# Moving value casts, a carry and a residual add in the issue order of a fused linear-attention and highway kernel

## The chip, the cores and the metric

The kernel runs on one core of a Trainium2 chip. The metric is the device time of one execution in microseconds (us); where several runs exist, their median.

## The reference

Eight batches of eight heads, 576 rows and 64 columns go through an attention without a score matrix, and the result through a highway layer of width 512:

```
q_s = exp(q) / sum over columns          (the maximum cancels)
k_s = exp(k) / sum over rows
kv  = k_s^T v                            (64 x 64 for each head)
x   = q_s kv                             (4608 x 512, heads side by side)
H   = max(x w_h, 0);  T = sigmoid(x w_t + b_t)
out = T*H + (1-T)*x
```

Inputs and output are float32; inside, the kernel works in float16 with float32 sums in PSUM.

## The kernel before, in words

**Tiles.** A batch lies in SBUF as 128 partitions by 4 head groups by 9 row blocks by 64 columns. Eight of the nine row blocks go through the highway layer batch by batch (column c = 0 to 7); the ninth blocks of all batches are collected and make two last columns of their own, c = 8 and 9. The layer works on transposed x, so each column has four output blocks ob = 0 to 3 of 128 features. Two batches form a pair g, whose rows leave the chip together.

**Steps of a batch b.** `exp_half` (L179, ScalarE) takes the exponential of half of q or k. `cast_v` (L189, GpSimd) converts half of the values to float16; batches 1 and 2 use `cast_v_head` (L197), a quarter at a time, on GpSimd and ScalarE. `q_sums` (L230, VectorE) sums exp(q) over the columns, half a batch at a time; `q_sums_tree` (L240) does the same by two adds and a shorter sum. `q_recip` (L251, VectorE) inverts the sums, and `q_scale_p` (L262, GpSimd) multiplies exp(q) by them, in two pieces (row blocks 0 to 3 and 4 to 8; batches 1 and 2 in three). The scaled q is turned by TensorE and copied back by VectorE (`q_trans`, L266, three pieces), for batches 6 and 7 by transposing DMAs on SP's queue (`q_turn`, L287). `kv_half` (L206, TensorE) forms k^T v, which needs the cast values and exp(k) but not the scaled q; `kv_norm` (L219, VectorE) normalizes it. `x_pair` (L331, TensorE, then a copy by ScalarE) needs both kv and the turned q.

**Steps of a block (c, ob).** `gate` (L375): four matmuls (`pt`), then tanh on ScalarE. `carry` (L386): four matmuls (`ph`), then one VectorE operation (`dd`, L401) that merges relu and x. `blend` (L406, VectorE, L409) multiplies the two. `pt` and `ph` share four PSUM banks, so a later gate or carry waits until an earlier `dd` or blend has read its bank. `add_x` (L417, at L421) adds x to the blended block on GpSimd; the blocks that `late` (L419) names are added on VectorE. `out_tile` (L436, eight per pair) turns the result back by one TensorE matmul for each block and, for blocks not in `added(g)` (L414), adds x by a second matmul.

**Order of the work.** No planner is at work: each engine executes in the order in which the program emits its instructions. The emission order is a list of start-up steps (L585), followed by `events` (L500), a table sorted by a hand-given position: block (c, ob) has its gate at 8c + 2ob, its carry at one more, its blend at two more. A batch b's steps stand around p = 8(b - 1), with offsets by batch (L543 to L579): `s0`, `s1` for the sums, `sc` for the scaling, `tr` for the turns, `kv`, and `x`. Steps of equal position keep the order of the source.

```
            s = p + {3: 0, 4: 0}.get(b, -0.5)
            at(s, E(exp_half, b, "k", 0), E(cast_v, b, 0))
            at(s + 0.9, E(cast_v, b, 1))
            at(s + 1, E(exp_half, b, "k", 1))
...
            4: ((3, 4, 4.9), (4.5, 4.5), (5.9, 6.9)),
...
        E(exp_half, 2, "q", 0), E(q_sums_tree, 2, 0), E(exp_half, 2, "q", 1),
        E(q_sums_tree, 2, 1), E(q_recip, 2),
```

Of the kernel before, what the change touches and what calls it, by code (L numbers as in the profile page):

```python
# [18 lines left out]
def kernel(  # L19
# [10 lines left out]
    nc = tc.nc  # L30
    B, H, S, D = q.shape
# [128 lines left out]
    def two_banks(name, dt=FP32):  # L160
        return ps_2.tile([P, 2, 2048 // (4 if dt is FP32 else 2)], dt, tag="q2", name=name)
# [202 lines left out]
    def views(c):  # L364
        if c >= B:
            h = slice(4 * (c - B), 4 * (c - B) + 4)
            return lambda k_: x9[:, k_, h], lambda k_: g9[:, k_, h]
        g, b2 = c // 2, c % 2
        if g not in gT:
            gT[g] = gp.tile([P, 4, NM, 2, 64], FP16, tag="g", name=f"g_{g}")  # L370
        return lambda k_: xT[g][:, k_, :, b2, :], lambda k_: gT[g][:, k_, :, b2, :]
# [39 lines left out]
        )  # L411


    added = lambda g: ((0, 1), (0, 1, 2), (0, 1, 2), (0, 1, 2, 3))[g]  # L414
    added9 = lambda g: (0, 1, 2, 3) if g < 2 else (0, 1)

    def add_x(c, ob):  # L417
        xv, gv = views(c)
        late = ob == (3 if c == B - 1 else 2) and c % 2 and c < B  # L419
        eng = nc.vector if late else nc.gpsimd  # L420
        eng.tensor_add(gv(ob), gv(ob), xv(ob))  # L421

# [79 lines left out]
    def at(p, *fs):  # L502
        events.setdefault(p, []).extend(fs)

    E = lambda f, *a: (lambda: f(*a))

    for c in range(1, B + 2):
        for ob in range(4):
            p = 8 * c + 2 * ob
# [6 lines left out]
    for g in range(B // 2):  # L516
        p = 16 * (g + 1)
# [6 lines left out]
    p = 8 * B + 8  # L524
# [1 line left out]
    at(p + 4, E(tile9, 1, 4))  # L526
    at(p + 8, E(tile9, 2, 3), E(tile9, 3, 3), E(last9))

    at(8, E(cast_v_head, 2, 0, nc.gpsimd), E(q_scale_p, 2, 0, 4), E(q_scale_p, 2, 4, 8))
    at(8.2, E(x_left, 1))  # L530
    at(16.2, E(x_left, 2))
    at(9, E(exp_half, 2, "k", 0))
    at(10, E(cast_v_head, 2, 1, nc.scalar), E(exp_half, 2, "k", 1))
    at(10.5, E(blend, 0, 3))
    at(12.5, E(add_x, 0, 0), E(add_x, 0, 1), E(add_x, 1, 0))
    at(14.5, E(add_x, 1, 1))
    for c in range(2, B + 2):
        for ob in added(c // 2) if c < B else added9(2 * (c - B)):
            at(8 * c + 2 * ob + (2.5 if c < B - 1 else 2.02), E(add_x, c, ob))
    at(11, E(cast_v_head, 2, 2, nc.gpsimd), E(cast_v_head, 2, 3, nc.scalar))  # L540
    at(11, E(q_scale_p, 2, 8, N9))
    for b in range(2, B):
        p = 8 * (b - 1)  # L543
        if b > 2:
            e0, e1, s0, s1, sc = {
                3: (-2.6, -1.6, -1.1, -0.1, 1),
                4: (-5.5, -4.5, -2.8, -1.5, -1.4),
                5: (-5, -4, -3.4, -2.7, -2.6),
                6: (-6, -5, -3.95, -3.1, -3),
                7: (-6, -5, -3.95, -3.1, -3),  # L550
            }.get(b, (-5, -4, -3.9, -2.9, -2.8))
            at(p + e0, E(exp_half, b, "q", 0))
            at(p + e1, E(exp_half, b, "q", 1))
            at(p + s0, E(q_sums, b, 0))
            at(p + s1, E(q_sums, b, 1), E(q_recip, b))
            at(p + sc, E(q_scale_p, b, 0, 4))
            at(p + sc + (0.6 if b > 5 else 0), E(q_scale_p, b, 4, N9))
            s = p + {3: 0, 4: 0}.get(b, -0.5)
            at(s, E(exp_half, b, "k", 0), E(cast_v, b, 0))
            at(s + 0.9, E(cast_v, b, 1))  # L560
            at(s + 1, E(exp_half, b, "k", 1))
        tr, kv, x = {
            2: ((5, 6, 7.1), (4, 6.2), (6.5, 7.2)),
            3: ((4, 4.9, 4.95), (4, 4), (5.9, 6.9)),
            4: ((3, 4, 4.9), (4.5, 4.5), (5.9, 6.9)),
        }.get(b, ((2, 3, 4), (4, 4), (5, 6)))
        if b in turned:
            at(p - 1.05, E(q_turn, b, 0, 4), E(q_turn, b, 4, N9))
        else:
            for i in range(3):  # L570
                home = (lambda: two_banks("pq_t", FP16)[:, 0]) if b < 4 and i == 2 else None
                at(p + tr[i], E(q_trans, b, i, home))
        at(p + kv[0], E(kv_half, b, 0))
        if b == 2:
            at(p + kv[0], E(kv_norm, b, 0, 1))
            at(p + kv[1], E(kv_half, b, 1), E(kv_norm, b, 1, 2))
        else:
            at(p + kv[1], E(kv_half, b, 1), E(kv_norm, b))
        homes = (nat_bank, single) if b == 2 else None  # L579
        at(p + x[0], E(x_pair, b, 0, "AA" if b == 2 else "A", b > 2, homes))  # L580
        at(p + x[1], E(x_pair, b, 1, "AV" if b == 2 else "A", b > 2, homes))
# [3 lines left out]
    for f in [  # L585
        E(warm_up, 24),
        E(exp_half, 0, "q", 0), E(q_sums, 0, 0),
        E(exp_half, 0, "q", 1), E(q_sums, 0, 1),
        E(q_recip, 0), E(q_scale_v, 0, 0, 4), E(q_scale_v, 0, 4, N9),
        E(exp_half, 0, "k", 0), E(cast_v, 0, 0),  # L590
        E(exp_half, 0, "k", 1), E(cast_v, 0, 1),
        E(q_trans, 0, 0), E(q_trans, 0, 1, lambda: two_banks("pq_0_1", FP16)[:, 0]), E(warm_up, 2), E(q_trans, 0, 2, lambda: nat_bank("pq_0_2", FP16)),
        E(warm_up, 6),
        E(kv_half, 0, 0), E(gate_bias), E(warm_up, 2), E(kv_half, 0, 1), E(kv_norm, 0),
        *[E(cast_weight, "t", k_, (nc.vector, nc.gpsimd)[k_ % 2]) for k_ in range(4)],
        E(warm_up, 4),
        E(x_pair, 0, 0, "AA"), E(warm_up, 2), E(x_pair, 0, 1, "AV", False, (ht_bank, ht_bank)), E(warm_up, 1), E(x_left, 0),
        E(exp_half, 1, "q", 0), E(q_sums_tree, 1, 0),
        E(exp_half, 1, "q", 1), E(q_sums_tree, 1, 1), E(q_recip, 1),
        *[f for k_ in range(4) for f in (E(less_one, k_), E(cast_weight, "h", k_, nc.scalar, 0.5))],  # L600
        E(q_scale_p, 1, 0, 4), E(q_scale_p, 1, 4, 8),
        E(gate, 0, 0), E(gate, 0, 1), E(gate, 0, 2, lambda: two_banks("pt_0_2")[:, 0]), E(warm_mid, 5),
        E(carry, 0, 0), E(blend, 0, 0), E(carry, 0, 1), E(exp_half, 1, "k", 0),
        E(gate, 0, 3, lambda: nat_bank("pt_0_3")), E(blend, 0, 1), E(carry, 0, 2),
        E(q_trans, 1, 0), E(blend, 0, 2), E(carry_products, 0, 3),
        E(exp_half, 1, "k", 1),
        *[E(cast_v_head, 1, c, (nc.scalar, nc.gpsimd, nc.gpsimd, nc.scalar)[c]) for c in range(4)],
        E(q_scale_p, 1, 8, N9),
        *[E(load, 2, w) for w in "qk"], E(load, 2, "v", [nc.sync, nc.sync]),
        *[E(load, 3, w) for w in "qkv"],  # L610
        E(q_trans, 1, 1), E(kv_half, 1, 0), E(kv_half, 1, 1), E(kv_norm, 1),
        E(q_trans, 1, 2), E(carry_diff, 0, 3),
        E(x_pair, 1, 0, "AV", False, (ht_bank, ht_bank)),
        E(x_pair, 1, 1, "AV", False, (ht_bank, one_of_two)),
        E(exp_half, 2, "q", 0), E(q_sums_tree, 2, 0), E(exp_half, 2, "q", 1),
        E(q_sums_tree, 2, 1), E(q_recip, 2),
    ]:
        f()
    for p in sorted(events):
# [32 lines left out]
```

The softmax here doesn't subtract the row's maximum and nothing guards it: scores larger than these inputs give would overflow.

## Time and profile before

| what | value |
| --- | --- |
| median of 11 runs | 130.78 us (130.06 to 131.89) |
| the profiled execution | 130.69 us, of which the span of its instructions is 128.9 us |
| granted TensorE clock | 0.99 |
| busy: TensorE (PE) / VectorE (DVE) / ScalarE (ACT) / GpSimd (POOL) | 112.0 / 99.5 / 92.3 / 77.9 us |
| x added by TensorE in `out_tile` | 32 matmuls `nat<-ident,xT` |
| x added by GpSimd, full blocks | 21 of 1152 ns |
| x added by VectorE, full blocks | 3 of 987 ns on average |
| two-piece scaling on GpSimd | 9 of 1902 ns (1024 elements), 5 of 2403 ns (1280) |
| cast of half a batch's values on GpSimd | 12 of 1146 ns |
| sum of half a batch on VectorE | 12 of 1344 ns |

How to read it: times count from the first instruction of the span. A row of a timeline gives start, duration, engine, source line, operation, output and input with shapes, and in brackets how long the engine was idle ahead of it and what it then waited for. A row with "x2" merges neighbours; neighbours on an engine overlap by some hundredths of a microsecond in the record. No engine is busy all the time, and the limit changes from stage to stage, so busy shares of the whole span decide little.

### The profile page before, as it was taken

How to read it: one execution, taken by the hardware profiler on the slowest of the kernel's cores; microseconds unless marked ns; L12 is line 12 of the kernel's file. 1: busy time of each engine (PE TensorE's matmuls, PEld its weight loads, DVE VectorE, ACT ScalarE, POOL GpSimd, SP SyncE). 2: the span in 40 equal slices, each digit the busy share in tenths (PEclk: the TensorE clock that was granted, in tenths of full speed). 3: DMA queues.
4: the chain of work that ended last, by engine and by line, in shares of the span. 5: the costliest groups of instructions: out<-in, count | busy, mean ns of one | idle time of the engine just before them, and what ended most of it. 6: DMA issues, size and time to landing. Idle time of an engine off the chain costs nothing.

```text
span 128.9 us, 3346 instructions
## 1 busy us (share of the span) xinstructions
PE 112.0 (87%) x1359; PEld 60.9 (47%) x1359; DVE 99.5 (77%) x181; ACT 92.3 (72%) x130; POOL 77.9 (60%) x73
## 2 busy tenths in 40 slices
PE   4998997986967899999769999995989999999950
PEld 2335442352435346555534555454435445579830
DVE  1297456898799999898689998983999656688970
ACT  3553059995998579779929995998797575757640
POOL 2003436790289999649955993699399746434510
PEclk9999999999999999999999999999999999999996
DMA  4999999999999999999999599999406906134994
GB/s 122 375 401 385 403 402 412 411 410 416 401 411 410 402 412 411 405 410 409 327 411 414 233 257 409 405 308 307 168 6 131 362 15 262 69 135 193 407 404 169
DMA packets 20583, 41.24 MB, mean 320 GB/s; under 512 B 5460, under 2 KB 5976, under 8 KB 19544
## 3 DMA queue, kind: packets, MB, share of 16 engines
q1 hardware_dynamic: 20568, 41.03, 85.4%
q8 instruction: 10, 0.16, 0.5%
q14 instruction: 5, 0.04, 0.1%
HBM read 30.41 MB, written 9.44 MB: 309 GB/s over the span
## 4 chain that ended last, share of the span: by engine, by line
DVE 25%; POOL 23%; PE 20%; DMA 11%; issue 8%; ACT 6%; SPq 3%; POOLq 0%; DVEq 0%; ACTq 0%
POOL eq L264 13%; DMA q<-in_q_dram 11%; DVE r L234 7%; PE ph L64 6%; PE pt L64 6%; POOL v L195 6%; DVE dd L401 5%; DVE g L409 4%; POOL g L421 4%; PE nat L64 3%; PE psk L64 2%; SPq L96 2%; DVE g L421 2%; PE pq L69 2%; ACT eq L183 2%
## 5 line engine op out<-in xcount | busy, mean ns | idle before, releaser
L264 POOL TENSOR_TENSOR eq<-eq,r 128x1024 f16<-128x1024 f16 (+2 forms) x16 | 30.1, 1897 | 10.6 <-DVE r L252 10.1
L64 PE MATMUL pt<-xT,w16t 128*128 128x512 f16 x128 | 33.6, 379 | 2.9 <-DVE dd L401 2.0
L64 PE MATMUL ph<-xT,w16h 128*128 128x512 f16 x128 | 33.3, 380 | 1.1 <-ACT w16h L116 0.7
L383 ACT ACTIVATE pt<-pt,bt 128x512 f32<-128x512 f32 (+1 forms) x40 | 24.7, 622 | 7.9 <-PE pt L64 7.4
L421 POOL TENSOR_TENSOR g<-g,xT 128x512 f16<-128x512 f16 x21 | 23.9, 1152 | 8.1 <-DVE g L409 8.1
L409 DVE SCALAR_TENSOR_TENSOR g<-pt,dd 128x512 f16<-128x512 f32 (+1 forms) x40 | 25.2, 633 | 2.9
L401 DVE SCALAR_TENSOR_TENSOR dd<-xT,ph 128x512 f16<-128x512 f16 x32 | 21.7, 677 | 4.5 <-PE ph L64 4.3
L64 PEld LDWEIGHTS <-w16t 128*128 128x128 f16 x160 | 14.7, 97 | 19.1 <-issue 6.6
L183 ACT ACTIVATE eq<-q 128x1152 f16<-128x1152 f32 x16 | 18.2, 1176 | 4.1 <-DMA q<-in_q_dram 4.0
L183 ACT ACTIVATE ek<-k 128x1152 f16<-128x1152 f32 x16 | 18.6, 1176 | 1.8 <-DMA k<-in_k_dram 1.8
L195 POOL CAST v<-v 128x1152 f16<-128x1152 f32 x12 | 13.5, 1146 | 10.1 <-DMA v<-in_v_dram 10.1
L64 PEld LDWEIGHTS <-w16h 128*128 128x128 f16 x160 | 13.6, 98 | 11.4 <-ACT w16h L116 2.4
L234 DVE TENSOR_REDUCE r<-eq 128x18 f32<-128x1152 f16 x12 | 16.0, 1344 | 3.8 <-ACT eq L183 3.7
L64 PE MATMUL nat<-ident,g 128*128 128x128 f16 x142 | 16.0, 219 | 0.7 <-DVE g L409 0.4
L64 PEld LDWEIGHTS <-g 128*128 128x128 f16 x144 | 12.5, 98 | 7.6 <-DVE g L409 1.1
L461 ACT COPY o<-nat 128x512 f32<-128x512 f32 x26 | 15.6, 601 | 0.0
L354 ACT CAST xT<-px 128x1024 f16<-128x1024 f32 x10 | 10.2, 1017 | 7.4 <-PE px L64 7.4
L64 PE MATMUL warm<-wide,ident 128*128 128x512 f16 x41 | 12.5, 452 | 1.8 <-DVE wide L153 1.8
L69 PE MATMUL pq<-ident,eq 128*128 128x128 f16 x104 | 8.5, 219 | 1.6 <-DVE qsT L282 1.1
L357 ACT CAST xT<-px 128x512 f16<-128x512 f32 x8 | 4.3, 590 | 7.8 <-PE px L64 7.8
L282 DVE COPY qsT<-pq 128x1024 f16<-128x1024 f16 (+1 forms) x16 | 9.3, 587 | 0.7 <-PE pq L69 0.2
L69 PEld LDWEIGHTS <-eq 128*128 128x128 f16 x108 | 6.9, 97 | 5.1 <-issue 1.9
(57 smaller groups left out, 107.8 us busy)
## 6 DMA issues: line engine op xcount, KB each, us to landing
out_dram<-o SPq DMA_DIRECT2D x8, 1024.0 KB, 4.8
q<-in_q_dram SPq DMA_DIRECT2D x7, 1152.0 KB, 13.6
k<-in_k_dram SPq DMA_DIRECT2D x7, 1152.0 KB, 13.2
v<-in_v_dram SPq DMA_DIRECT2D x5, 1152.0 KB, 13.7
v<-in_v_dram SPq DMA_DIRECT2D x6, 576.0 KB, 11.7
q<-in_q_dram SPq DMA_DIRECT2D x2, 576.0 KB, 4.0
k<-in_k_dram SPq DMA_DIRECT2D x2, 576.0 KB, 7.1
w32t<-in_moe_w_t_dram SPq DMA_DIRECT2D x1, 1024.0 KB, 11.2
```

The lines of the kernel that those rows point to most:

```text
L64: mm = lambda o, l, r, st, sp: nc.tensor.matmul(o, l, r, start=st, stop=sp, skip_group_check=True)
L69: nc.tensor.matmul(o, i, ident, is_transpose=True, start=True, stop=True, skip_group_check=True,)
L183: nc.scalar.activation(dst[b][:, :, 2 * a : 2 * a + 2, :], in32[which][b][:, 2 * a : 2 * a + 2].rearrange("p c n d -> p n c d"), AF.Exp,)
L195: (eng or nc.gpsimd).tensor_copy(o, i)
L234: nc.vector.reduce_sum(qsum[b][:, :, h], eq[b][:, :, h, :], axis=AX.X)
L264: nc.gpsimd.tensor_mul(e, e, r.broadcast_to(list(e.shape)))
L354: copy[how](dst, t2.rearrange("p c (n d) -> p c n d", d=64))
L383: nc.scalar.activation(ps, ps, AF.Tanh, bias=bt2[:, ob : ob + 1], scale=0.5)
L401: nc.vector.scalar_tensor_tensor(dd, xv(ob), -0.5, ps, op0=ALU.mult, op1=ALU.max)
L409: nc.vector.scalar_tensor_tensor(gv(ob), th, 1.0, dd, op0=ALU.add, op1=ALU.mult)
L421: eng.tensor_add(gv(ob), gv(ob), xv(ob))
L461: nc.scalar.copy(o, flat(t))
```

## The change

Six edits, all of order except the last:

1. `q_sums_tree(2, 1)`, `q_recip(2)` and the first two pieces of `q_scale_p(2)` move from the end of the start-up list and from position 8 to position 9.05. The x copies of `x_left(1)` (8.2) and the carry of block (1, 0) (9) now precede them.
2. `cast_v` of batches 4 to 7, both halves, moves from behind `q_scale_p` of the same batch (positions s and s + 0.9) to just ahead of it (sc - 0.02), behind that batch's `q_recip` in the emission order.
3. The sums and the scaling of batch 5 move from offsets -3.4, -2.7, -2.6 to -2.95, -2.2, -2.1, so both sums come after the carry of block (3, 2).
4. `kv_half` and `kv_norm` of batch 4 move from 4.5 to 4.95, behind the last piece of `q_trans(4)`.
5. `added(2)` grows from three blocks to four: for pair 2 (batches 4 and 5) x is added to all blocks outside TensorE.
6. `late` takes every ob from 2 on (for batch 7, from 3 on as before), so block (5, 3) is added on VectorE and block (4, 3) on GpSimd.

```diff
-    added = lambda g: ((0, 1), (0, 1, 2), (0, 1, 2), (0, 1, 2, 3))[g]
+    added = lambda g: ((0, 1), (0, 1, 2), (0, 1, 2, 3), (0, 1, 2, 3))[g]
...
-        late = ob == (3 if c == B - 1 else 2) and c % 2 and c < B
+        late = c % 2 and c < B and ob >= (3 if c == B - 1 else 2)
...
-    at(8, E(cast_v_head, 2, 0, nc.gpsimd), E(q_scale_p, 2, 0, 4), E(q_scale_p, 2, 4, 8))
+    at(8, E(cast_v_head, 2, 0, nc.gpsimd))
+    at(9.05, E(q_sums_tree, 2, 1), E(q_recip, 2), E(q_scale_p, 2, 0, 4), E(q_scale_p, 2, 4, 8))
...
-                5: (-5, -4, -3.4, -2.7, -2.6),
+                5: (-5, -4, -2.95, -2.2, -2.1),
...
-            at(s, E(exp_half, b, "k", 0), E(cast_v, b, 0))
-            at(s + 0.9, E(cast_v, b, 1))
+            at(s, E(exp_half, b, "k", 0))
             at(s + 1, E(exp_half, b, "k", 1))
+            if b > 3:
+                at(p + sc - 0.02, E(cast_v, b, 0), E(cast_v, b, 1))
+            else:
+                at(s, E(cast_v, b, 0))
+                at(s + 0.9, E(cast_v, b, 1))
...
-            4: ((3, 4, 4.9), (4.5, 4.5), (5.9, 6.9)),
+            4: ((3, 4, 4.9), (4.95, 4.95), (5.9, 6.9)),
...
-        E(q_sums_tree, 2, 1), E(q_recip, 2),
```

## The prediction, made before the changed kernel ran

> **What bounds the kernel now.** I read the chain that ended last, then the busy time by stage, then each engine's timeline. The stage table (columns: stretch, its length, busy time with instruction counts of PE, PEld, DVE, ACT, POOL; clock; DMA share; GB/s):
>
> ```profile
> 35.80:53.70 17.90, 15.71 (x257) 8.42 (x257) 16.85 (x33) 14.51 (x20) 17.90 (x14) 1.00 1.04 410
> 69.27:82.04 12.77, 12.17 (x163) 6.57 (x162) 11.85 (x18) 11.43 (x16) 9.24 (x7) 1.00 0.92 327
> 82.04:93.84 11.80, 10.25 (x140) 5.41 (x140) 9.02 (x14) 10.45 (x15) 9.69 (x8) 1.00 0.91 273
> 104.32:113.00 8.68, 8.59 (x57) 4.62 (x56) 5.72 (x9) 5.34 (x9) 4.10 (x4) 1.00 0.30 125
> ```
>
> From 35.8 to 53.7 us POOL has no idle time. From 69 to 82 PE and DVE are both close to full. From 104 on PE alone is. The POOL timeline:
>
> ```profile
> 34.65 0.66 POOL L203 CAST v<-v 128x576 f16<-128x576 f32 x1 [5.67 <-PE pt L64]
> 35.79 3.76 POOL L264 TENSOR_TENSOR eq<-eq,r 128x1024 f16<-128x1024 f16 x2 [0.48 <-DVE x L315]
> ...
> 47.30 4.19 POOL L264 TENSOR_TENSOR eq<-eq,r 128x1024 f16<-128x1024 f16 x2
> ...
> 57.77 4.19 POOL L264 TENSOR_TENSOR eq<-eq,r 128x1024 f16<-128x1024 f16 x2 [0.62 <-DVE r L252]
> 61.90 2.23 POOL L195 CAST v<-v 128x1152 f16<-128x1152 f32 x2
> ...
> 69.27 4.37 POOL L264 TENSOR_TENSOR eq<-eq,r 128x1024 f16<-128x1024 f16 x2 [2.91 <-DVE r L252]
> ```
>
> Each scaling waits for a reciprocal and the cast follows it. Whether a cast fits into the idle time ahead of a scaling is read here: 0.62 us for batch 4, 2.91 for batch 5. TensorE's waits that the edits aim at, and one VectorE add:
>
> ```profile
> 36.63 1.02 PE L64 MATMUL pt<-xT,w16t 128*128 128x512 f16 x4 [1.24 <-DVE dd L401]
> ...
> 51.55 0.62 PE L69 MATMUL pq<-ident,eq 128*128 128x128 f16 x8
> ...
> 88.05 0.48 PE L64 MATMUL psk<-v,ek 64*64 64x65 f16 x36 [0.69 <-POOL v L195]
> 89.14 0.48 PE L64 MATMUL psk<-v,ek 64*64 64x65 f16 x36 [0.61 <-POOL v L195]
> ```
>
> ```profile
> 69.67 1.77 DVE L421 TENSOR_TENSOR g<-g,xT 128x512 f16<-128x512 f16 x1
> ...
> 114.32 0.42 DVE L421 TENSOR_TENSOR g<-g,xT 128x512 f16<-128x512 f16 x1
> ```
>
> **What the Trainium skill says.** "SBUF — State Buffer", section "SBUF: two separate sides": GpSimd and a VectorE operation with two SBUF inputs take a shared port pair as an exclusive lock for a whole instruction. The trace agrees: the same add takes 0.42 us with POOL idle and 1.77 us when it starts 0.4 us into a scaling, ending when that piece ends. "GPSIMD Engine Reference", section "4.1 Engine selection": two-input elementwise work is about twice as slow there; here 1.152 us against 0.42, more than that. "TensorE: Matmul & The Clock Gate", section "Wait — 56ns, not 53.3ns?", gives about 56 ns between matmuls; in the chain here five `nat` matmuls take 0.28 us, 56 each.
>
> **Edit 1, carry before the second sum of batch 2.** It removes PE's 1.24 us wait: `dd`(1,0) runs at about 34.3 instead of 35.90. But the tree (1.23 us), and with it the reciprocal, comes later: x copies 0.34 + `dd` 0.60 = 0.94 us. The tree's first add has two SBUF inputs and would meet the value cast at 34.65 to 35.31, so I add 0.3 for the lock; the scaling of batch 2 starts at 35.79 + 1.23 = 37.03. (Ends: 0.85 without lock, 1.25.) Queued behind it on POOL are a cast, a third piece, four adds, the cast of batch 3 and its scaling, 11.51 us without a gap, so batch 3's scaling starts at 48.54 and ends at 52.73. TensorE's second turn of batch 3 (51.55 now, 0.06 us after the scaling's end at 51.49) starts at 52.78; behind it stand carry (2,2), x of batch 3 and everything else. **+1.23 at 53 us.** PE's won 1.24 us is lost again, as DVE is 94% busy here (16.85 of 17.90) and POOL full.
>
> **Edits 2 to 4 in stage 3 (batch 4).** On POOL the cast (2.20) now lies between add (2,2) and the scaling. Add (2,2) still waits for its blend: 56.01 + 1.23 = 57.24. Then 1.10 add + 2.20 cast: scaling at 60.54, its halves done at 62.44 and 64.73 (before 59.66 and 61.96). PE is ready for the first turn at 60.58 + 1.23 = 61.81 and waits 0.7; the second waits until 64.78; the third waits for the one PSUM bank, 0.66 + 0.65 us more, 66.1. Then kv 0.8 (values long cast), carry (3,2) 0.86: x of batch 4 at 67.83, against 66.88: +0.95, so the values' waits of 0.25 + 0.61 and the 1.13 behind the copy turn into three waits of the same size. VectorE loses more. Before, sum (5,0) filled a wait; now both sums (2.53) follow `dd`(3,2): 67.88 + 0.60 + 2.53 = 71.03, reciprocal done at 71.41, before 69.10: **+2.3**, 1.07 of it new. Bounds of that: 0, if the sums still slip into idle time, to 1.5. Blend (3,2), its VectorE add and `dd`(3,3) follow, and gate (4,1) waits for that bank (72.43, 0.05 after `dd`): 74.7. Batch 5's cast is hidden in the 2.91 us idle time; without that cover it would add 2.2 to the scaling.
>
> **Stage 4.** DVE's only idle time is 0.47 us, ahead of `kv_norm`(5), and that waits for TensorE, which waited for DVE's copies. No slack: +2.3 persists to gate (5,0), 84.3.
>
> **Stage 5, where the cast pays.** Batch 6's reciprocal comes at 83.75; its cast runs before, 80.6 to 82.8. PE's kv 6 takes 0.78 us instead of 2.35 (87.20 to carry (5,2) at 89.55): **-1.57** (ends -1.3, the two waits, and -1.6). x of batch 6 then needs the DMA transposes: scaling ends at 88.1, and the second transpose, issued then, lands after 3.1 to 5.0 us, 3.4 in the middle: 91.5, where PE is ready at 91.24. Their issue on SP has only a store behind it. +1.0 here.
>
> **Stage 6.** POOL's queue up to batch 7's scaling gains add (4,3), 1.10, and the cast, 2.20: free at 94.7, the reciprocal at 93.96. VectorE add (5,2) at 95.55 meets the first piece (till 96.6) and ends at 96.95, 1.4 later than before; the new add (5,3), ready at 98.3, meets the second (till 98.9): bounds 0.42 and 2.4 us, I take 1.0. Gate (6,2) waits for `dd`(6,0), 99.9 instead of 98.25. kv 7 saves 0.2. x of batch 7: about **+1.4**, so this stage adds 0.7 to stage 5's net +0.73 (bounds 0 to 1.2). The transposes (102.2) come earlier than that (102.8).
>
> **Edits 5 and 6 at the end.** Eight `nat` matmuls go, 8 x 56 ns = 0.45 us of PE. Four lie in the TensorE-bound stretch 104 to 112: -0.22. The last precedes a wait for add (7,3), the others lie next to waits (ends 0 and -0.45). Add (4,3)'s result is needed at 97 us at the earliest: the add itself is hidden.
>
> **Sum.** 1.23 + 1.07 - 1.57 + 0.7 - 0.22 = +1.2 us against the profiled 130.69: **131.9 us**; the profiled time is 0.09 under the median. Lower ends together: 0.85 + 0 - 1.6 + 0 - 0.45 = -1.2; upper: 1.25 + 1.5 - 1.3 + 1.2 = +2.65.
>
> **Rivals.** (a) **Faster**: the delays of batches 2 and 4 are absorbed by idle time between 53 and 70 that I hold for dependent waits (DVE 13.76 of 15.57 us, PE 13.54), and only the value waits go. kv 6 -1.57, kv 7 -0.2, `nat` -0.22, x of batch 4 -0.28, with +0.85 left of edit 1: -1.4, 129.3 us. For it: TensorE idles 2.0 us in stage 3 today. Against: POOL's unbroken 17.90 us. It decides at batch 5's reciprocal: at 70 us or earlier, this rival wins. (b) **No change**: edit 1 costs 0.85, batch 5's sums 0.6, the adds on VectorE meet no piece: 0.85 + 0.6 - 1.57 + 0.2 - 0.22 = -0.1, 130.6 us. (c) **The transposes become the bound**: delayed behind loads (5.0 us to landing, as the first piece of batch 6 is) at both batches, 0.8 us each: 133.5. That the edits do nothing is excluded: they fix each engine's order.
>
> **Chances.** Forecast 0.52, (a) 0.20, (b) 0.22, (c) 0.06. A measurement tells about 0.5% (0.65 us) from no change. Of the forecast's own 131.2 to 132.9, nearly all is slower (0.50), (c) all (0.06), (b) mostly the same (0.17, rest on both sides), (a) faster (0.19): faster 0.21, same 0.20, slower 0.59. The range goes from 129.6, near (a), to 133.1, the upper bounds without (c).
>
> **What would show it.** In the changed trace: gate (1,2) at 35.3 without a wait; scaling of batch 2 at 36.7 to 37.1 and of batch 3 at 48.2 to 48.6; the second turn of batch 3 waiting for POOL; the scaling of batch 4 behind its cast, near 60.5; batch 5's reciprocal near 71.4; no wait for values at kv 6 and 7; VectorE adds (5,2) and (5,3) each over 0.9 us; 24 `nat<-ident,xT` matmuls. The forecast is wrong if batch 3's scaling isn't later, or if gate (4,1) comes within 1 us of 72.4.

## The result, and the profile after

The changed kernel takes 132.69 us (median of 12 runs, 131.88 to 134.86), the kernel before 130.80 (median of 47): **ratio 1.0152, interval 1.0126 to 1.0178**, about 2.0 us slower. The forecast was 131.9. Ratios here leave out executions more than 1.5% above the fastest of their kernel, which are one of these 12, and two of the six with only the casts of batches 6 and 7 moved.

The profiled execution of after took 132.95 us, span 131.1. It started later than the one of before: batch 1's q landed later, and the first sum of batch 2, which no edit touches, starts at 33.38 us instead of 32.75. So 0.63 us has to be taken off each difference between the two traces; I call what is left "aligned". The traces of the experiments are aligned in the same way, each at its own first sum of batch 2.

GpSimd (POOL) after, in the stretch of batches 2 to 5:

```profile
37.46 3.76 POOL L264 TENSOR_TENSOR eq<-eq,r 128x1024 f16<-128x1024 f16 x2 [1.70 <-DVE r L252]
...
48.98 4.18 POOL L264 TENSOR_TENSOR eq<-eq,r 128x1024 f16<-128x1024 f16 x2
...
58.58 2.23 POOL L195 CAST v<-v 128x1152 f16<-128x1152 f32 x2
60.78 4.18 POOL L264 TENSOR_TENSOR eq<-eq,r 128x1024 f16<-128x1024 f16 x2
...
72.20 4.37 POOL L264 TENSOR_TENSOR eq<-eq,r 128x1024 f16<-128x1024 f16 x2 [2.84 <-DVE r L252]
```

Batch 2's scaling has 1.70 us of idle time ahead of it instead of 0.48. Batch 3's is 1.68 later than before (aligned 1.05), batch 4's, now behind its cast, 3.01 (2.38), batch 5's 2.93 (2.30).

TensorE (PE) after:

```profile
35.85 1.03 PE L64 MATMUL pt<-xT,w16t 128*128 128x512 f16 x4
...
53.22 0.62 PE L69 MATMUL pq<-ident,eq 128*128 128x128 f16 x8 [0.94 <-POOL eq L264]
...
62.73 0.62 PE L69 MATMUL pq<-ident,eq 128*128 128x128 f16 x8 [0.45 <-POOL eq L264]
...
65.02 0.62 PE L69 MATMUL pq<-ident,eq 128*128 128x128 f16 x8 [0.47 <-POOL eq L264]
66.42 0.27 PE L69 MATMUL pq<-ident,eq 128*128 128x128 f16 x2 [0.78 <-DVE qsT L282]
```

```profile
75.36 1.02 PE L64 MATMUL pt<-xT,w16t 128*128 128x512 f16 x4 [1.66 <-DVE dd L401]
...
90.22 0.78 PE L64 MATMUL psk<-v,ek 64*64 64x65 f16 x72
...
92.22 0.22 PE L64 MATMUL px_l<-qsD,kvn 64*64 64x64 f16 x2 [0.25 <-DMA qsD<-eq]
...
100.04 0.23 PE L64 MATMUL nat<-ident,g 128*128 128x128 f16 x1 [0.69 <-DVE g L421]
...
100.97 1.03 PE L64 MATMUL pt<-xT,w16t 128*128 128x512 f16 x4
```

Gate (1,2) at 35.85 has lost its wait of 1.24 us, and the second turn of batch 3 at 53.22 has got one of 0.94 for GpSimd. Batch 4's turns wait three times. Gate (4,1) at 75.36 waits 1.66 us for `dd`(3,3). kv of batch 6 at 90.22 runs in one piece, without its waits for values. The row at 100.04 is a wait that the forecast had not named: the first out tile of pair 2 now needs the block that VectorE adds late. The last row is gate (6,2). VectorE (DVE) at that place:

```profile
96.23 1.29 DVE L421 TENSOR_TENSOR g<-g,xT 128x512 f16<-128x512 f16 x1
...
98.94 1.04 DVE L421 TENSOR_TENSOR g<-g,xT 128x512 f16<-128x512 f16 x1
99.91 0.67 DVE L401 SCALAR_TENSOR_TENSOR dd<-xT,ph 128x512 f16<-128x512 f16 x1
```

The two adds are those of blocks (5,2) and (5,3), the third row is `dd`(6,0). Each add ends just after a piece of batch 7's scaling (pieces 95.34 to 97.24 and on to 99.71): at 97.52 and 99.98.

### The profile page after: what moved, and what is told of

Same layout as the page of the kernel before. It is cut to its first block, busy times and chain, and to the rows that moved or that the text cites. A ratio compares the mean times of both kernels' runs of the same rounds, so it can differ in the third digit from the quotient of the medians.

```text
span 131.1 us, 3334 instructions
## 1 busy us (share of the span) xinstructions
PE 111.1 (85%) x1351; PEld 59.9 (46%) x1351; DVE 101.3 (77%) x182; ACT 92.6 (71%) x130; POOL 79.1 (60%) x74
## 4 chain that ended last, share of the span: by engine, by line
DVE 27%; PE 25%; POOL 16%; DMA 11%; issue 8%; ACT 6%; SPq 3%; DVEq 0%; POOLq 0%; ACTq 0%
DMA q<-in_q_dram 11%; POOL eq L264 8%; PE ph L64 8%; PE pt L64 8%; DVE r L234 6%; DVE dd L401 6%; DVE g L409 5%; POOL g L421 5%; PE nat L64 4%; DVE g L421 3%; PE psk L64 3%; POOL v L195 3%; SPq L96 2%; PE pq L69 2%; ACT eq L183 1%
## 5 line engine op out<-in xcount | busy, mean ns | idle before, releaser
L421 POOL TENSOR_TENSOR g<-g,xT 128x512 f16<-128x512 f16 x22 | 25.0, 1149 | 12.5 <-DVE g L409 12.5
L64 PE MATMUL nat<-ident,g 128*128 128x128 f16 x142 | 15.7, 219 | 1.4 <-DVE g L421 1.0
L64 PE MATMUL warm<-wide,ident 128*128 128x512 f16 x41 | 11.6, 427 | 1.8 <-DVE wide L153 1.8
```

The costliest lines, as they stand in the source:

```text
L64: mm = lambda o, l, r, st, sp: nc.tensor.matmul(o, l, r, start=st, stop=sp, skip_group_check=True)
```

## The experiments

All ratios are to the kernel before, run beside them; "us" is the ratio's distance from 1 times the median of before in those runs (130.82 or 130.74).

**Edit 1 alone.**

```diff
-    at(8, E(cast_v_head, 2, 0, nc.gpsimd), E(q_scale_p, 2, 0, 4), E(q_scale_p, 2, 4, 8))
+    at(8, E(cast_v_head, 2, 0, nc.gpsimd))
+    at(9.05, E(q_sums_tree, 2, 1), E(q_recip, 2), E(q_scale_p, 2, 0, 4), E(q_scale_p, 2, 4, 8))
...
-        E(q_sums_tree, 2, 1), E(q_recip, 2),
```

> Kernel before with edit 1 alone (second sum tree, reciprocal and scaling of batch 2 behind the x copies and the carry of block (1,0)). Forecast's theory: GpSimd has no slack from batch 2's scaling to batch 3's, so the later start (about +1.0 us) is passed whole to batch 3's second turn on TensorE, and nothing later gives it back: +0.9 to +1.2 us on the time. First rival (the loss comes from the VectorE adds, edits 5 and 6): 0. Second rival (the 1.24 us that TensorE wins at gate (1,2) pays for it): -0.3 to +0.3.

Measured: 1.0077 (1.0034 to 1.0121), +1.0 us. GpSimd and TensorE in this run:

```profile
37.03 3.76 POOL L264 TENSOR_TENSOR eq<-eq,r 128x1024 f16<-128x1024 f16 x2 [1.70 <-DVE r L252]
...
48.53 4.19 POOL L264 TENSOR_TENSOR eq<-eq,r 128x1024 f16<-128x1024 f16 x2
```

```profile
35.38 1.03 PE L64 MATMUL pt<-xT,w16t 128*128 128x512 f16 x4
...
52.77 0.62 PE L69 MATMUL pq<-ident,eq 128*128 128x128 f16 x8 [0.96 <-POOL eq L264]
```

From one scaling to the other it is 11.50 us, as before (47.30 - 35.79 = 11.51): the late start is carried through unchanged to batch 3's scaling, and TensorE gives back at batch 3's second turn what it won at gate (1,2). Aligned (this trace starts 0.16 us later than before), batch 3's scaling is 1.07 us late, and 0.87 us of it are left at gate (5,0), 83.07 against 82.04. Both rivals fall.

**Edit 1 undone**, all else as in the changed kernel.

> Changed kernel with edit 1 undone. Forecast's theory: about half of the loss goes, +0.8 to +1.1 us against before; batch 3's scaling again starts 11.5 us after batch 2's, which starts right after the second x exponential. First and second rivals: the loss stays at +1.8 to +2.1 us.

Measured: 1.0053 (1.0012 to 1.0094), +0.7 us. What stays is just under the 0.8 to 1.1 us of the forecast's theory, which lie within this run's interval (0.2 to 1.2 us). Of the 2.0 us about 1.3 goes; the intervals of edit 1's two shares (1.0 added alone, 1.3 on removal) overlap.

**Edits 5 and 6 alone** (`added` and `late`). Both change which engine adds x to a block, not the order.

> Kernel before with edits 5 and 6 alone (fourth block of pair 2 added off TensorE; block (5,3) on VectorE). Forecast's theory: 0.2 us of TensorE time won in the last stages, and against it the VectorE add (5,3) that waits for batch 7's scaling piece and holds up the first out tile of pair 2; in the old order about 0.5 us of that hides in batch 7's wait for values: +0.0 to +0.5 us. First rival (these adds are the loss): +1.3 us or more.

Measured: 1.0005 (0.9961 to 1.0050), no change that can be told; a cost of up to 0.65 us would lie within the interval. The add (5,3) took 1.05 us in this trace too, and the out tile waited for it:

```profile
96.16 1.05 DVE L421 TENSOR_TENSOR g<-g,xT 128x512 f16<-128x512 f16 x1
...
97.27 0.23 PE L64 MATMUL nat<-ident,g 128*128 128x128 f16 x1 [0.69 <-DVE g L421]
```

Aligned (this trace starts 0.86 us earlier than before), carry (6,1) is 0.80 us late. At x of batch 7 it is 0.51, mainly because kv of batch 7 takes 0.71 us instead of 0.94 up to the carry behind it: values that it used to wait for are there by now. At the end, with the matmuls less, 0.26 us are left.

**Casts ahead for batches 6 and 7 only.**

```diff
+            if b > 5:
+                at(p + sc - 0.02, E(cast_v, b, 0), E(cast_v, b, 1))
+            else:
+                at(s, E(cast_v, b, 0))
+                at(s + 0.9, E(cast_v, b, 1))
```

> Kernel before with edit 2 for batches 6 and 7 only (casts ahead of the scaling where GpSimd waits for the reciprocal anyway). Forecast's theory: kv of batch 6 no longer waits for values (1.3 us) and of batch 7 (0.2 us); the transposes of batch 6 take back at most 0.3 us: -1.0 to -1.5 us, faster than before. Rival (the transposing DMAs or VectorE's sums take the place of the value wait at once): -0.3 to +0.3 us.

Measured: 0.9875 (0.9823 to 0.9926), -1.6 us, for the four executions of 128.43 to 130.04 us: there this part of the change is a gain, and the rival falls. The other two took 132.24 and 132.65 us, and the kept trace is of the first of these:

```profile
87.42 0.78 PE L64 MATMUL psk<-v,ek 64*64 64x65 f16 x72
...
91.45 0.22 PE L64 MATMUL px_l<-qsD,kvn 64*64 64x64 f16 x2 [2.28 <-DMA qsD<-eq]
```

kv of batch 6 waits for no values, but its x waits 2.28 us for the transposing DMA and starts 0.8 us later than before (90.51, aligned). In this execution what the rival describes did happen. No trace of one of the four was kept, and why the DMA landed late here is open.

**The stage of batches 4 and 5 alone.**

```diff
-                5: (-5, -4, -3.4, -2.7, -2.6),
+                5: (-5, -4, -2.95, -2.2, -2.1),
...
+            if 3 < b < 6:
+                at(p + sc - 0.02, E(cast_v, b, 0), E(cast_v, b, 1))
...
-            4: ((3, 4, 4.9), (4.5, 4.5), (5.9, 6.9)),
+            4: ((3, 4, 4.9), (4.95, 4.95), (5.9, 6.9)),
```

> Kernel before with the stage of batches 4 and 5 alone: edit 2 for batches 4 and 5, edit 3 (sums of 5 later) and edit 4 (kv of 4 later). Forecast's theory: TensorE's waits for values turn into waits for the later scaling of batch 4, and both sums of batch 5 now follow carry (3,2), so batch 5's reciprocal comes about 1.1 us later and the time with it: +0.9 to +1.2 us. Rival (removing the value wait of batch 4 helps, the lateness of the sums is absorbed): -0.5 to +0.2 us.

Measured: 1.0117 (1.0089 to 1.0144), +1.5 us, more than expected and of the sign expected. VectorE in this run:

```profile
64.38 0.69 DVE L282 COPY qsT<-pq 128x1024 f16<-128x1024 f16 x1 [1.00 <-PE pq L69]
65.44 0.29 DVE L282 COPY qsT<-pq 128x256 f16<-128x256 f16 x1 [0.36 <-PE pq L69]
66.17 0.18 DVE L222 RECIPROCAL rz<-psk 128x4 f32<-128x4 f32 x1 [0.44 <-PE psk L64]
66.39 0.42 DVE L223 TENSOR_TENSOR kvn<-psk,rz 128x256 f16<-128x256 f32 x1
67.11 0.69 DVE L401 SCALAR_TENSOR_TENSOR dd<-xT,ph 128x512 f16<-128x512 f16 x1 [0.30 <-PE ph L64]
67.72 2.60 DVE L234 TENSOR_REDUCE r<-eq 128x18 f32<-128x1152 f16 x2
70.36 0.38 DVE L252 RECIPROCAL r<-r 128x36 f32<-128x36 f32 x1
```

VectorE stands idle 2.1 us in four waits for TensorE, and only then comes 2.60 us of sums. The reciprocal starts at 70.36. Before, it was here, and behind it gate (4,1):

```profile
68.72 0.38 DVE L252 RECIPROCAL r<-r 128x36 f32<-128x36 f32 x1
```

```profile
72.43 1.02 PE L64 MATMUL pt<-xT,w16t 128*128 128x512 f16 x4
```

Aligned (this trace starts 0.17 us later than before), the reciprocal is 1.47 us late, and gate (5,0), 83.69 against 82.04, still 1.48.

**The same without edit 3**: casts of 4 and 5 ahead, kv of 4 later, the sums of 5 at their old place.

> As the run of batches 4 and 5, with edit 3 left out: the sums of batch 5 stay at their old place, ahead of the last copy of batch 4. Forecast's theory: sum (5,0) fills a wait of VectorE again, batch 5's reciprocal is back near its old time: +0.0 to +0.3 us. Rival (the late scaling of batch 4 is what costs, not the place of the sums): +0.8 to +1.2 us, as with edit 3.

Measured: 1.0002 (0.9973 to 1.0030), no change: the 1.5 us go with one line. VectorE here, and gate (4,1):

```profile
63.94 0.69 DVE L282 COPY qsT<-pq 128x1024 f16<-128x1024 f16 x1 [1.00 <-PE pq L69]
64.55 1.34 DVE L234 TENSOR_REDUCE r<-eq 128x18 f32<-128x1152 f16 x1
65.81 0.28 DVE L282 COPY qsT<-pq 128x256 f16<-128x256 f16 x1
...
66.67 0.69 DVE L401 SCALAR_TENSOR_TENSOR dd<-xT,ph 128x512 f16<-128x512 f16 x1
67.28 1.34 DVE L234 TENSOR_REDUCE r<-eq 128x18 f32<-128x1152 f16 x1
68.66 0.38 DVE L252 RECIPROCAL r<-r 128x36 f32<-128x36 f32 x1
```

```profile
72.37 1.02 PE L64 MATMUL pt<-xT,w16t 128*128 128x512 f16 x4 [0.28 <-DVE dd L401]
```

The first sum fills the time in which VectorE stood idle three times above, and the reciprocal is back at 68.66. The late scaling of batch 4 is there in both runs, so it isn't what the 1.5 us are paid for, and the rival falls. That the late scaling costs nothing is not shown: this run also holds edit 4, which is a gain in the last run below, so the two may offset each other.

**Edits 5 and 6 undone**, all else as in the changed kernel.

> Changed kernel with edits 5 and 6 undone (three blocks of pair 2 added off TensorE, only block (5,2) on VectorE). Theory after the result: no wait of the first out tile of pair 2 for add (5,3), batch 7's scaling a little earlier, against eight more TensorE matmuls: 0.5 to 1.0 us under the changed kernel, +1.0 to +1.5 us against before. Rival (the adds are free here as they were alone): +1.9 to +2.2 us against before.

Measured: 1.0059 (1.0034 to 1.0084), +0.8 us: the adds cost about 1.2 us in the new order (1.0152 against 1.0059), a little more than expected, and nothing that can be told in the old one. The trace of this run has the first VectorE add at 0.77 us, as in the kernel before, and no wait of the out tile. At batch 6's scaling this trace is 1.35 us ahead of after (83.20 against 84.55), and with that taken off, gate (6,1) is 0.5 us apart (96.29 against 98.17) and carry (6,1) 1.3 (97.43 against 100.11). The first 0.5 us is the longer add (5,2), 1.29 us instead of 0.77, behind a scaling that add (4,3) had pushed back on GpSimd by 0.53 us; the other 0.8 is the out tile's wait.

**Casts of 6 and 7, and edit 4.** As the run of the casts alone, with kv of batch 4 at 4.95.

> Kernel before with edit 2 for batches 6 and 7 only and edit 4 (kv of batch 4 behind its last turn). Theory: the last turn of batch 4 no longer queues behind kv's wait for values, its x no longer waits 1.1 us for the copy behind a sum, and batch 5's reciprocal comes 0.7 to 0.9 us earlier: another 0.6 to 1.0 us under the run with the casts alone, -2.1 to -2.6 us against before. Rival (kv of batch 4 still waits for its values, and what follows is no earlier): as the casts alone, -1.2 to -1.7 us.

Measured: 127.99 us, 0.9786 (0.9751 to 0.9822), **-2.8 us: faster than both kernels**, by somewhat more than expected. TensorE in this run, and one row of VectorE:

```profile
71.39 1.02 PE L64 MATMUL pt<-xT,w16t 128*128 128x512 f16 x4 [0.33 <-DVE dd L401]
...
86.25 0.78 PE L64 MATMUL psk<-v,ek 64*64 64x65 f16 x72
...
88.40 0.22 PE L64 MATMUL px_l<-qsD,kvn 64*64 64x64 f16 x2 [0.40 <-DMA qsD<-eq]
```

```profile
67.69 0.38 DVE L252 RECIPROCAL r<-r 128x36 f32<-128x36 f32 x1
```

kv of batch 6 waits for no values; what waits next is its x, 0.40 us for the transposing DMA. The reciprocal of batch 5 starts at 67.69 us, 1.03 earlier than before, since kv of batch 4 no longer holds up the last turn.

So edit 4, on top of the casts of 6 and 7, is worth about 1.2 us (-2.8 against -1.6; gate (4,1) comes 1.08 us earlier than before, aligned). Gate (4,1) starts at 71.39 here and at 72.37 in the run without edit 3, where the cast of batch 4 stands ahead of its scaling: aligned (0.04 us later and 0.28 us earlier than before), 1.30 us apart. My estimate from these two rows is that this cast takes back all that edit 4 wins.

Two things have no measurement. One is the adds beside the casts of 6 and 7, in the otherwise old order (-0.5 to -1.1 us was expected against before): that the cover of the adds was batch 7's wait for values is read from the traces, not shown by a run of its own. The other is the cast ahead of batch 4's scaling by itself.

## Why the prediction was right, and where it was short

**The sign and the mechanism held.** Gate (1,2) without a wait, batch 3's second turn waiting for POOL, batch 4's scaling behind its cast, gate (4,1) late and kv of 6 and 7 without waits all appear.

| step | forecast | measured |
| --- | --- | --- |
| edit 1 | +1.23 (0.85 to 1.25) | +1.05 aligned at batch 3's scaling; +1.0 as a run of its own |
| batch 5's reciprocal, total | +2.3 | +2.30 aligned |
| the stage of 4 and 5 by itself | +1.07 (0 to 1.5) | +1.25 aligned (2.30 less 1.05); +1.5 as a run |
| kv of batch 6 | -1.57 | -1.56 aligned (2.94 at gate (5,0) to 1.38 at carry (5,2)) |
| carry (5,2) to x of batch 7 | +0.7 (0 to 1.2) | +1.05 aligned |
| `nat` matmuls at the end | -0.22 | -0.23 (2.43 at x of batch 7, 2.2 at the span's end) |

**Edit 1** was 0.2 too dear. I had added 0.3 us for the tree's first add meeting the value cast under the lock, from an overlap of 0.42 us (34.89 to 35.31). In the trace of after the two overlap by 0.18 us only:

```profile
35.09 0.66 POOL L203 CAST v<-v 128x576 f16<-128x576 f32 x1 [5.48 <-DMA v<-in_v_dram]
```

```profile
35.57 0.50 DVE L245 TENSOR_TENSOR t<-eq 128x576 f16<-128x576 f16 x1
```

Aligned, the cast starts 0.19 us earlier than before and the add 0.05 us later than forecast. The add takes 0.50 us, 0.46 elsewhere. The x copies and `dd` (0.39 + 0.60 in this trace) and 0.04 in the add make up 1.03 of the 1.04 us by which batch 2's scaling is late. The lock itself held. The page of the Trainium skill that I took it from ("SBUF — State Buffer", section "SBUF: two separate sides") counts every GpSimd operation that reads SBUF, and the traces agree for a cast, with one input, too: with edit 1 alone the overlap is 0.22 us and the add takes 0.54, so in both traces the add ends 0.32 us after the cast. In the run with the adds undone it is the cast that is held up, by the tree's second add, and takes 0.79 us instead of 0.66:

```profile
34.76 0.31 DVE L246 TENSOR_TENSOR t<-t 128x288 f16<-128x288 f16 x1
```

```profile
34.80 0.79 POOL L203 CAST v<-v 128x576 f16<-128x576 f32 x1 [6.34 <-PE ph L64]
```

**The stage of batches 4 and 5** was forecast at 1.07 and measures 1.5 as a run. The forecast named the sums' place ("VectorE loses more"), and leaving edit 3 out removes all 1.5. What it did not have apart is that edit 4 is a gain as long as the cast of batch 4 stays where it was, and that this cast seems to take it back: it saw there three waits that turn into three others of the same size. Of edit 1's 1.05 us only 0.87 are left at gate (5,0), so that of the 2.31 us there (2.94 less 0.63) this stage holds rather 1.44 than 1.25.

**The adds are the step that was mis-sized.** The forecast said that add (4,3) is hidden, and didn't ask the same of add (5,3): the first out tile of pair 2 (position 50) reads that block, only one carry and one gate lie between it and the add (48.5), and TensorE's carry (6,1) stands behind the tile. Of add (5,3) the forecast priced only the delay of the next `dd`, and that came out: it had add (5,2) end at 96.95 and gate (6,2) start at 99.9, held by `dd`(6,0), which is done at 99.95 aligned (99.91 + 0.67 - 0.63). But gate (6,2) starts at 100.34 aligned (100.97 - 0.63), behind the out tile's 0.69 us wait and carry (6,1). So of the 0.69 us about 0.35 to 0.4 is new loss, an estimate from these rows, and that is the step's gap (1.05 against 0.7). Removing the adds gives back 1.2 us, where the forecast's terms that hold them come to some 0.5 (0.7 less 0.22).

**The whole.** Aligned, the traces differ by 2.2 - 0.63 = 1.6 us, the medians by 1.9, the ratio says 2.0. By the table, the forecast's +1.2 lacks 0.35 in stage 6 and 0.2 in the stage of 4 and 5, and has 0.2 too much in edit 1; the two last cancel by luck. The rest, 0.1 to 0.8 us by the ratio's interval, is not assigned to a step. Part of it may be that starts vary from one execution to the next, which two traces can't average. One sum of the forecast is off: its upper ends (+2.65 on 130.69) come to 133.3, not 133.1.

**The rivals.** (a), delays absorbed between 53 and 70 us, fell at its own test: batch 5's reciprocal is done at 72.03, 71.40 aligned, not by 70. Its gain at kv 6 is real, as the casts of 6 and 7 alone show. (b), no change, had 0.6 us for batch 5's sums and VectorE adds that meet no piece; the sums cost 1.5 and both adds met one. (c) was seen in the changed kernel as a wait of 0.25 us at batch 6, no more, but as one of 2.28 us in an execution with the casts of 6 and 7 alone.

## What to carry to other kernels

A step that an engine's queue holds up is worth moving only into time in which that engine would stand idle: the casts of batches 6 and 7 went into waits for a reciprocal and gained 1.6 us in four executions of six, while a carry moved ahead of a sum won 1.24 us on TensorE and lost all of it on a GpSimd queue that had no gap for 15.7 us. The cast of batch 4 went ahead of a scaling with 0.62 us of idle time in front of it, and seems to have taken back what a later kv won. Ask of each moved filler what idle time it used to fill: sum (5,0) had covered a wait for free and cost 1.5 us as soon as it stood behind it. For an operation given to another engine, check its first reader as well as its length.

## What the runs showed of the hardware that was not expected

- A VectorE add with two SBUF inputs that meets a piece of GpSimd's two-input scaling ends 0.27 to 0.29 us after that piece (it takes 1.77, 1.29, 1.05 or 1.04 us against 0.42 alone). The forecast had it end with the piece: at 71.44 before, the piece ends at 71.17.
- A GpSimd cast, with one input, and a VectorE add with two hold each other up in the same way. The add took 0.50 us with 0.18 us of overlap and 0.54 with 0.22, against 0.46. The cast took 0.79, 0.76 and 0.73 us when it started 0.27, 0.23 and 0.21 us before the add's end (the runs with the adds undone, of batches 4 and 5, and with the casts of 6 and 7), and 0.66 us when it started 0.10 before it (the kernel before). In these rows the one that comes second loses the overlap less about 0.14 us.
- The landing of batch 1's q moved whole executions: its exponential started between 17.9 and 19.6 us in these traces, with nothing changed ahead of it. Two traces should be aligned at a step that no edit touches before they are subtracted.
